# Scaling the features of linear attention on ScalarE or VectorE instead of GpSimd, with new due times for attention units, weights and raw unpacks

## The chip, the core and the metric

The kernel is one program on one core of a Trainium2 chip. The engines of a core run on their own and wait for one another by semaphores: TensorE (PE in the rows, PEld for its weight loads), VectorE (DVE), ScalarE (ACT), GpSimd (POOL) and SyncE (SP), which here issues the DMAs. The metric is device time in microseconds of one execution. Each engine works through its own list of instructions strictly in order.

## The reference

Three stages follow one another, all in float32. First linear attention with random features, over 4 batches and 8 heads of 576 tokens with 64 columns:

```python
def phi(x):                                   # 128 features
    proj = np.einsum('bhsd,md->bhsm', x, omega)
    h = proj - np.sum(x * x, axis=-1, keepdims=True) / 2.0
    h = h - np.max(h, axis=-1, keepdims=True)
    return np.exp(h) / np.sqrt(m)
kv = np.einsum('bhsm,bhsd->bhmd', k_p, v)
z = np.sum(k_p, axis=2)
num = np.einsum('bhsm,bhmd->bhsd', q_p, kv)
den = np.einsum('bhsm,bhm->bhs', q_p, z)[..., None] + 1e-06
return num / den
```

Its output becomes 2304 tokens of 512 columns. Then come two feed-forward layers, 512 to 2048 to 512 columns each: the first with `g = max(0.01 h, h)`, the second with `g = h * clip(h + 3, 0, 6) / 6`.

## The kernel before

**Tiling.** The 2304 tokens are worked on in five groups, 512, 256, 512, 512 and 512 tokens. Attention is cut into units: a K unit (`K_unit`) makes the key side of one batch and one pair of heads, a Q unit (`Q_unit`) the output of some tokens of one batch for one to four pairs of heads. Group 0's attention runs first. After that the first layer of a group (`moe1`) fills TensorE, and the units of later groups are slipped in between its matmuls, up to about 330 us. The rest of the time belongs to the two layers: float32 products made of three matmuls of split operands (L520, L521, L522), and in the second layer seven products in place of eight (L1199 for its hidden values, L1096 for its output).

**A Q unit.** Scores on TensorE (L775) give one bank of up to four blocks of 128 tokens by 128 features. VectorE takes minima (L740) and corrects them (L743, L745), ScalarE makes the exponentials into a tile `h` (L750), VectorE the denominators (L942) and their reciprocals (L948). Then `h` is scaled by the reciprocals, which stand one to a token, that is one to a partition and block: the step of this change, the op behind `sc` at L953. TensorE transposes the scaled blocks (L968), ScalarE or VectorE copies them out as `tq`, and a last product with `kvf` (L999) gives the output, copied to `xr`.

**A K unit.** Scores and exponentials as above, then `kvt` (L842) into a bank, copied out as `kvf`, transposed on TensorE (L849), copied again. Beside it the sums over tokens: GpSimd or VectorE adds halves of the `h` tiles in place (L509), then the 64 tokens left over (L862), and TensorE spreads the sum over the partitions (L866) for a copy to `zr`.

**Weights of the first layer.** They arrive packed and are unpacked by ScalarE (L550, L554) and VectorE (L552, L557, L560, L563). Each unpacked tile is split in a rounded part and a rest: a cast on ScalarE (L501) or GpSimd (L570), and a subtraction on VectorE (L504) or GpSimd (L505).

**What sets the order.** The code hands every step to a graph as an op with a due time, an estimated cost and one or more alternatives, each an engine with its cost. `Graph.run` then writes the program: it picks, over and over, the op that can start first by its own books, the one due earlier where two are close, and on the alternative that ends first. For ops of attention on TensorE a number is added to the time from which they may go: `WAIT` by the kind of op where the last matmul was one of the first layer's, `MATE` where it was itself a score ("S") or a 64-column product ("N"), `FOLLOW` behind an "F" op. The due time of an attention unit is its place in its group's stretch plus an entry of `MOVE_A` times 100 ns; `MOVE_W` does the same for the weights of the first layer, `MOVE_R` for the unpacking of the second layer's weights, which is done ahead of time. None of these numbers is in the program that runs; they decide only in which order, and on which engine, its instructions stand.

The op that scales, as it stands, with its two alternatives and their costs:

```python
g.op([("dve", c_dve(w), lambda sc=sc: sc(nc.vector), True), ("pool", 150 + w * 1.85, lambda sc=sc: sc(nc.gpsimd))],
     rd=[den], wr=[h], due=due + 4e3)
```

Of the kernel before, what the change touches and what calls it, by code (L numbers as in the profile page):

```python
# [13 lines left out]
AF = mybir.ActivationFunctionType  # L14
# [5 lines left out]
B, H, S, D = 4, 8, 576, 64  # L20
# [15 lines left out]
ST1, ST2 = 2, 2  # L36
SLACK = 1.0
PACE = 2.215
WAIT = {"S": 2250.0, "N": 1650.0, "F": 1300.0}
FOLLOW = 160.0  # L40
MATE = 60.0
TURN = {("M", "S"): 193.0, ("M", "N"): 92.0, ("S", "M"): 205.0, ("N", "M"): 158.0, ("F", "S"): 193.0, ("F", "N"): 97.0, ("S", "F"): 175.0,
        ("N", "F"): 150.0, ("S", "N"): 97.0, ("N", "S"): 150.0, ("F", "M"): 8.0}
OLDKV = 1
# [7 lines left out]
T0 = 42000.0  # L52
L1 = [100000.0, 52000.0, 127000.0, 87e3, 87e3]
ATT = [None, (32000.0, 132000.0), (132e3, 170000.0), (182e3, 244000.0), (220e3, 260000.0)]
MOVE_A = [[3, 9, -6, -16, 1, 25, 4, 21, 18],
# [4 lines left out]
MOVE_W = [-92, -14, -44, 44, 0, -14, 76, 43, -6, -11, -19, 86, -6, 15, -14, 7, 1, 28, 3, -3, -98, 56, 0, 18, -96, 40, 27, 0, 0, -1, 47, 0]  # L60
MOVE_R = [0, 26, -85, 43, -11, 44, 10, 154, 0, 0, 0, -67, 18, 42, -47, -62, 12, -5, -71, 66, 0, 106]
RAW = (142000.0, 302000.0)
PREP = (315000.0, 400000.0)
EARLYX = [0, 2, 3]
# [277 lines left out]
def c_dve(n):  # L342
    return n / 0.96 + 69.0
# [6 lines left out]
def c_act(n, psum=False, ap=False):  # L350
    return n / 1.2 + (51.0 if psum else 93.0) + (93.0 if ap else 0.0)
# [15 lines left out]
def attn_moe_kernel(ctx: ExitStack, tc: tile.TileContext, qT, kT, qn, kn, v1, om2, w1i, w1o, w2i, w2o, out):  # L367
# [4 lines left out]
    nc = tc.nc  # L372
    scale = float(D) ** -0.25
    g = Graph()
# [544 lines left out]
    def Q_unit(grp, b, hps, f, half, s0, col0, o, due):  # L919
        n, nh = f * 128 + 64 * half, len(hps)  # L920
        ncol, N, F = 2 * f + half, nh * n, f * 128
# [12 lines left out]
        for bank, (h, c) in enumerate(zip(hs, cols)):  # L934
            den, jk = Buf("den"), Buf("junk")
# [3 lines left out]
            def dn(h=h, den=den, jk=jk, heads=heads):  # L939
                for q, (k, _, e) in enumerate(heads):  # L940
# [8 lines left out]
                 wr=[den], due=due + 4e3)  # L949

            def sc(eng, h=h, den=den, c=c):
                x = h.tiles[0][:, 0:c * 128].rearrange("p (c f) -> p c f", f=128)
                eng.tensor_tensor(out=x, in0=x, in1=den.tiles[1][:, 0:c].to_broadcast([128, c, 128]), op=ALU.mult)  # L953

            w = c * 128
            g.op([("dve", c_dve(w), lambda sc=sc: sc(nc.vector), True), ("pool", 150 + w * 1.85, lambda sc=sc: sc(nc.gpsimd))],
                 rd=[den], wr=[h], due=due + 4e3)

            def tr(h=h, heads=heads):
                for q, (k, i, e) in enumerate(heads):  # L960
# [13 lines left out]
             wr=ts, also=[tq], due=due + 5e3)  # L974
# [5 lines left out]
        elif f:  # L980
            g.op(copy_alts(lambda: tq.tiles[0][:, :, 0:N], lambda: ts[0].tiles[0].rearrange("p (e n) -> p e n", e=2)[:, :, 0:N], 2 * N, True),
                 rd=[ts[0]], wr=[(tq, 0)], due=due + 5e3)
# [500 lines left out]
```

## Time and profile before

| what | value |
|---|---|
| median of three runs | 859.67 us (859.39 to 860.69) |
| the profiled execution | 860.87 us, its span 859.1 us |
| granted TensorE clock | 0.999 of full speed |
| TensorE matmuls | busy 849.7 us, 99%, 6279 of them |
| VectorE | busy 664.2 us, 77% |
| ScalarE | busy 511.0 us, 59% |
| GpSimd | busy 193.9 us, 23% |

Busy time says how long an engine had an instruction in work, not that someone waited for it. Who waited for whom is in two other views: the chain of the work that ended last, followed back from the end of the program, and the list of each engine's idle times with what ended them. A timeline row gives the start in us, the duration in us, engine, line and operation, the tiles (output first) and their shapes, how many instructions were put together, and in brackets the idle time before it with what ended it.

### The profile page before, as it was taken

How to read it: one execution, taken by the hardware profiler on the slowest of the kernel's cores; microseconds unless marked ns; L12 is line 12 of the kernel's file. 1: busy time of each engine (PE TensorE's matmuls, PEld its weight loads, DVE VectorE, ACT ScalarE, POOL GpSimd, SP SyncE). 2: the span in 40 equal slices, each digit the busy share in tenths (PEclk: the TensorE clock that was granted, in tenths of full speed). 3: DMA queues.
4: the chain of work that ended last, by engine and by line, in shares of the span. 5: the costliest groups of instructions: out<-in, count | busy, mean ns of one | idle time of the engine just before them, and what ended most of it. 6: DMA issues, size and time to landing. Idle time of an engine off the chain costs nothing.

```text
span 859.1 us, 18037 instructions
## 1 busy us (share of the span) xinstructions
PE 849.7 (99%) x6279; PEld 778.0 (91%) x6279; DVE 664.2 (77%) x1725; ACT 511.0 (59%) x1161; POOL 193.9 (23%) x279
## 2 busy tenths in 40 slices
PE   9999999999999999999999999999999999999998
PEld 8987888889888878888888889999999999999998
DVE  5999898966997965666889757886678779868765
ACT  6988797886877655544654455544443554345442
POOL 0125563333225321000100002122002223322110
PEclk9999999999999999999999999999999999999999
DMA  9566563766558416999888829986896784686441
GB/s 337 180 188 220 190 207 124 254 220 201 178 170 265 141 63 207 332 337 325 321 269 293 281 74 296 316 284 218 297 329 211 232 276 148 193 289 216 155 145 46
DMA packets 110250, 193.83 MB, mean 226 GB/s; under 512 B 13520, under 2 KB 46416, under 8 KB 110160
## 3 DMA queue, kind: packets, MB, share of 16 engines
q1 hardware_dynamic: 110016, 192.55, 68.1%
q8 instruction: 50, 0.82, 0.4%
q14 instruction: 40, 0.33, 0.1%
q10 hardware_dynamic: 144, 0.13, 0.1%
HBM read 148.60 MB, written 44.04 MB: 224 GB/s over the span
## 4 chain that ended last, share of the span: by engine, by line
PE 92%; DVE 3%; DMA 2%; ACT 1%; POOL 1%; issue 1%; DVEq 0%; POOLq 0%; SPq 0%; ACTq 0%
PE bank L1096 19%; PE bank L1199 17%; PE bank L520 15%; PE bank L522 14%; PE bank L521 14%; PE bank L775 4%; PE bank L999 2%; PE bank L842 2%; PE bank L968 1%; DVE junk L942 1%; PE bank L820 1%; PE bank L894 1%; DMA late_w<-in 1%; PE bank L866 1%; PE bank L1397 1%; DMA first_xn<-kn 1%
## 5 line engine op out<-in xcount | busy, mean ns | idle before, releaser
L501 ACT COPY late_u<-bank 128x256 f32<-128x256 f32 (+1 forms) x94 | 36.4, 387 | 79.0 <-PE bank L1199 74.6
L1096 PE MATMUL bank<-w,g 128*128 128x256 f32 x612 | 80.8, 275 | 0.0
L1096 PEld LDWEIGHTS bank<-w,g 128*128 128x128 f32 x612 | 74.4, 192 | 0.1
L1199 PE MATMUL bank<-w,late_w 128*128 128x256 f32 x546 | 72.9, 275 | 0.9 <-DMA late_w<-in 0.9
L1038 DVE TENSOR_TENSOR g<-bank,g 128x512 fp32r<-128x512 f32 (+1 forms) x80 | 50.4, 634 | 29.4 <-ACT g L501 28.5
L750 ACT ACTIVATE h<-bank,nm 128x128 f32<-128x128 f32 x228 | 63.7, 391 | 14.2 <-DVE nm L745 9.3
L1199 PE MATMUL bank<-x,late_w 128*128 128x256 f32 x540 | 69.3, 275 | 0.0
L1199 PEld LDWEIGHTS bank<-w,late_w 128*128 128x128 f32 x546 | 67.0, 192 | 1.3 <-DMA late_w<-in 1.1
L520 PE MATMUL bank<-x,w 128*128 128x512 f32 (+1 forms) x180 | 67.1, 373 | 0.0
L520 PE MATMUL bank<-g,w 128*128 128x512 f32 (+1 forms) x180 | 67.0, 372 | 0.0
L1199 PEld LDWEIGHTS bank<-x,late_w 128*128 128x128 f32 x540 | 64.9, 192 | 0.2
L1036 ACT ACTIVATE bank<-bank 128x512 f32<-128x512 f32 (+1 forms) x80 | 44.1, 553 | 34.8 <-PE bank L522 34.5
L522 PE MATMUL bank<-g,w 128*128 128x512 f32 (+1 forms) x180 | 64.6, 359 | 0.2 <-DVE g L1038 0.2
L522 PE MATMUL bank<-x,w 128*128 128x512 f32 (+1 forms) x180 | 64.6, 359 | 0.0
L521 PE MATMUL bank<-x,w 128*128 128x512 f32 (+1 forms) x180 | 64.5, 358 | 0.0
L521 PE MATMUL bank<-g,w 128*128 128x512 f32 (+1 forms) x180 | 64.5, 358 | 0.0
L1096 PE MATMUL bank<-second_w,g 128*128 128x256 f32 x453 | 59.9, 275 | 0.0
L740 DVE TENSOR_REDUCE nm<-bank 128x4 f32<-128x512 f32 (+2 forms) x76 | 47.2, 656 | 11.1 <-PE bank L775 9.9
L1096 PEld LDWEIGHTS bank<-second_w,g 128*128 128x128 f32 x453 | 55.2, 192 | 0.0
L501 ACT COPY u<-bank 128x256 f32<-128x256 f32 (+1 forms) x59 | 24.2, 412 | 51.8 <-PE bank L1199 30.8
L953 POOL TENSOR_TENSOR h<-h,den 128x512 f32<-128x512 f32 (+2 forms) x32 | 33.1, 1038 | 71.8 <-DVE den L948 44.0
L504 DVE TENSOR_TENSOR g<-xr,g 128x512 fp32r<-128x512 f32 (+1 forms) x55 | 36.7, 667 | 11.5 <-ACT g L501 10.4
(394 smaller groups left out, 2375.4 us busy)
## 6 DMA issues: line engine op xcount, KB each, us to landing
late_w<-in SPq DMA_DIRECT2D x207, 256.0 KB, 3.9
in<-late_w SPq DMA_DIRECT2D x64, 256.0 KB, 3.8
third_w<-in SPq DMA_DIRECT2D x49, 256.0 KB, 4.0
wst<-w2i SPq DMA_DIRECT2D x16, 512.0 KB, 4.7
wst<-w2o SPq DMA_DIRECT2D x16, 512.0 KB, 4.3
x_t<-late_w SPq DMA_DIRECT2D x12, 512.0 KB, 4.6
wst<-w1o SPq DMA_DIRECT2D x11, 512.0 KB, 3.6
v<-v SPq DMA_DIRECT2D x14, 330.0 KB, 4.2
```

The source lines that it names most:

```text
L501: return [("act", c_act(n, psum), lambda: nc.scalar.copy(dst(), src())), dve if psum else dve + (True,)]
L504: return [("dve", c_dve(n), lambda: nc.vector.tensor_tensor(out=dst(), in0=src(), in1=hi().bitcast(F32), op=ALU.subtract), True), ("pool", ...
L520: nc.tensor.matmul(o, lhsT=ah, rhs=bh, start=start, stop=False)
L521: nc.tensor.matmul(o, lhsT=al, rhs=bh, start=False, stop=False)
L522: nc.tensor.matmul(o, lhsT=ah, rhs=bl, start=False, stop=stop)
L740: g.op([("dve", c_dve(c * 128), lambda raw=raw, n_=n_: nc.vector.tensor_reduce(out=n_()[:, :, 0], in_=raw(), axis=AX.X, op=ALU.min))], rd= ...
L750: nc.scalar.activation(h.tiles[0][:, q * 128:q * 128 + 128], raw()[:, q], AF.Exp, bias=nm.tiles[0][:, q], scale=-1.0)
L775: nc.tensor.matmul(ps[e].tiles[0][:, at:at + 128], lhsT=src.tiles[0][r, k * one + i * 128:k * one + i * 128 + 128], rhs=wn[r], start=True, ...
L1036: g.op([("act", c_act(n, True), lambda: nc.scalar.activation(P(), P(), AF.Prelu, alpha=0.01))], wr=[p], due=d)
L1038: g.op([("dve", c_dve(n), lambda: nc.vector.tensor_tensor(out=G1(), in0=P(), in1=G0().bitcast(F32), op=ALU.subtract))], rd=[p, (gg, 0)], w ...
L1096: nc.tensor.matmul(acc[bank].tiles[0][:, half * 256:half * 256 + 256], lhsT=src.tiles[x][:, q * 128:q * 128 + 128], rhs=woven(w[k].tiles[y ...
L1199: nc.tensor.matmul(R[r](), lhsT=w[x], rhs=m[y], start=start and k == n == 0, stop=k == 1 and n == 2, skip_group_check=True)
```

## The change

The scaling gets a new second alternative. In place of GpSimd, which scaled the whole tile by one instruction with a broadcast operand, ScalarE may do it by one activation (`Copy` with a scale per partition) for each 128 columns. VectorE's alternative stays. Three constants of the planner and all of `MOVE_A`, `MOVE_W` and `MOVE_R` get other values; two rows of `MOVE_A` stand here for the rest.

```diff
-WAIT = {"S": 2250.0, "N": 1650.0, "F": 1300.0}
+WAIT = {"S": 1850.0, "N": 1600.0, "F": 1350.0}
 FOLLOW = 160.0
-MATE = 60.0
+MATE = 520.0
...
-MOVE_A = [[3, 9, -6, -16, 1, 25, 4, 21, 18],
-          [-30, 9, -29, 9, 9, -9, -79, 38],
+MOVE_A = [[-124, -103, -86, -78, -48, 31, -14, 4, -2],
+          [-31, -4, -37, 2, -6, -12, 0, -28],
...
-            g.op([("dve", c_dve(w), lambda sc=sc: sc(nc.vector), True), ("pool", 150 + w * 1.85, lambda sc=sc: sc(nc.gpsimd))],
-                 rd=[den], wr=[h], due=due + 4e3)
+            def by_act(h=h, den=den, c=c):
+                for q in range(c):
+                    x = h.tiles[0][:, q * 128:q * 128 + 128]
+                    nc.scalar.activation(x, x, AF.Copy, scale=den.tiles[1][:, q])
+
+            g.op([("dve", c_dve(w), lambda sc=sc: sc(nc.vector), True), ("act", c * c_act(128, True, True), by_act)], rd=[den], wr=[h], due=due + 4e3)
```

Of the 32 scalings, all on GpSimd before, 26 are on ScalarE now, as 90 activations (L959), and 6 on VectorE (L953). The lines behind the new function stand four further down: L968 is L972, L999 is L1003, L1038 is L1042, L1096 is L1100, L1199 is L1203. The number of matmuls is the same.

In the rows below the names carry slot and copy numbers: `w7_90` is slot 7 of the first layer's split weights, `late_w0_1` a weight tile of the second layer that is fetched while the layer runs.

First, SyncE's queue for the second layer, at about 594 us in the trace of before. Before:

```order
L693 DMA late_w0_1_0_3819<-in_3_0_256_243 128x512
L693 DMA late_w0_1_0_3819<-in_3_1_0_244 128x512
L525 DMA xr1_0_113<-x1_4_0_77 128x2x256
L693 DMA late_w0_2_0_3820<-in_3_1_256_245 128x512
L693 DMA third_w2_0_0_1645<-in_3_2_0_246 128x512
L525 DMA late_xr3_1_0_3829<-x1_4_0_77 128x2x256
L525 DMA xr3_0_115<-x1_4_1_78 128x2x256
L693 DMA late_w0_0_0_3818<-in_3_3_256_249 128x512
```

and of the changed kernel:

```order
L693 DMA late_w0_1_0_3883<-in_3_0_256_243 128x512
L525 DMA xr1_0_113<-x1_4_0_77 128x2x256
L525 DMA late_xr3_1_0_3893<-x1_4_0_77 128x2x256
L693 DMA late_w0_1_0_3883<-in_3_1_0_244 128x512
L693 DMA late_w0_2_0_3884<-in_3_1_256_245 128x512
L693 DMA third_w2_0_0_1691<-in_3_2_0_246 128x512
L525 DMA xr3_0_115<-x1_4_1_78 128x2x256
L693 DMA late_w0_0_0_3882<-in_3_3_256_249 128x512
```

The loads of `xr1` and `late_xr3` moved ahead of the second fetch into `late_w0_1`; the rest of the piece kept its order.

Second, GpSimd's queue around the first K unit of group 1, at about 60 to 70 us in the trace of before; a minus marks rows of before, a plus rows of the changed kernel:

```order
 L505 TENSOR_TENSOR w5_88<-first_wt6_1_0_175,w5_88 128x512
-L953 TENSOR_TENSOR h0_0_145<-h0_0_145,den2_1_193 128x512
-L505 TENSOR_TENSOR w6_89<-wt0_0_110,w6_89 128x512
+L570 CAST w6_89<-wt0_0_110 128x512
 L570 CAST w7_90<-wt1_0_111 128x512
+L570 CAST w8_91<-first_wt6_0_0_174 128x512
+L570 CAST w9_92<-first_wt6_1_0_175 128x512
 L509 TENSOR_TENSOR h1_0_146<-h1_0_146 128x256
 L509 TENSOR_TENSOR h2_0_147<-h2_0_147 128x256
```

A scaling and a subtraction ahead of the K unit's additions are gone from GpSimd, and three casts stand there beside the one of before.

Third, TensorE at the K unit that makes `kvf2`. Before, the last rows ahead of its transpose, of which the unit's `kvt` (L842) stands five rows above the first:

```order
L521 MATMUL bank6_182<-x1_102,w12_95 128x256
L522 MATMUL bank6_182<-x1_102,w12_95 128x256
L520 MATMUL bank6_182<-x2_103,w12_95 128x256
L521 MATMUL bank6_182<-x2_103,w12_95 128x256
L522 MATMUL bank6_182<-x2_103,w12_95 128x256
L520 MATMUL bank6_182<-x3_104,w12_95 128x256
L521 MATMUL bank6_182<-x3_104,w12_95 128x256
L522 MATMUL bank6_182<-x3_104,w12_95 128x256
L520 MATMUL bank0_176<-g0_105,w11_94 128x256
L521 MATMUL bank0_176<-g0_105,w11_94 128x256
L522 MATMUL bank0_176<-g0_105,w11_94 128x256
L849 MATMUL bank4_180<-ident_184,kvf2_0_130 128x128
```

and of the changed kernel:

```order
L842 MATMUL bank3_179<-h1_0_146,v0_0_144 64x128
L842 MATMUL bank3_179<-h2_0_147,v0_0_144 64x128
L842 MATMUL bank3_179<-ht0_0_152,v0_0_144 64x128 x2
L1003 MATMUL bank0_176<-tq0_0_154,kvf1_0_129 64x384 x2
L849 MATMUL bank3_179<-ident_184,kvf2_0_130 128x128
L520 MATMUL bank5_181<-g2_107,w9_92 128x256
```

Between `kvt` and the transpose of its result stood fifteen matmuls of the first layer, and now one group of two.

Fourth, ScalarE's queue at the same place in the changed kernel:

```order
L501 COPY tq0_0_154<-bank3_179 128x384
L1040 ACTIVATE bank0_176<-bank0_176 128x256
L501 CAST g0_105<-bank0_176 128x256
L554 ACTIVATE wt1_0_111<-wst1_0_109 128x512
L550 ACTIVATE wst1_0_109<-wst1_0_109 128x512
L501 COPY kvf2_0_130<-bank3_179 128x128
```

The copy that the transpose reads, `kvf2`, has two unpacking steps of a weight directly ahead of it.

## Rows read from the trace of the kernel before

**Rows 1.** The chain that ended last, share of the span by engine.

```profile
PE 92%; DVE 3%; DMA 2%; ACT 1%; POOL 1%; issue 1%; DVEq 0%; POOLq 0%; SPq 0%; ACTq 0%
```

**Rows 2.** TensorE's waits: line, releaser, total us, times, longest us.

```profile
PE bank L1199 <- DMA late_w<-in: 0.9, 1, 0.9
PE bank L1096 <- DVE late_g L504: 0.5, 1, 0.5
PE bank L849 <- ACT kvf L501: 0.4, 1, 0.4
...
PE bank L522 <- DVE g L1038: 0.2, 1, 0.2
PE bank L520 <- ACT tq L501: 0.2, 1, 0.2
```

**Rows 3.** Busy us (instructions) by stretch: PE, PEld, DVE, ACT, POOL, clock, DMA, GB/s.

```profile
58.00:160.00 102.00, 101.35 (x643) 84.35 (x642) 93.08 (x225) 86.68 (x194) 49.38 (x55) 1.00 0.59 191
...
592.00:594.00 2.00, 2.00 (x21) 2.00 (x20) 1.23 (x4) 1.65 (x3) 0.00 (x0) 1.00 0.54 186
```

**Rows 4.** The group of scalings: count, busy us, mean ns, idle before and its releaser.

```profile
L953 POOL TENSOR_TENSOR h<-h,den 128x512 f32<-128x512 f32 (+2 forms) x32 | 33.1, 1038 | 71.8 <-DVE den L948 44.0
```

**Rows 5.** ScalarE groups from 55 to 300 us, and one timeline row of eight exponentials.

```profile
L750 ACT ACTIVATE h<-bank,nm 128x128 f32<-128x128 f32 x188 | 52.4, 387 | 12.6 <-DVE nm L745 8.6 <-DVE nm L743 3.8
...
L554 ACT ACTIVATE wt<-wst 128x512 f32<-128x512 f32 x26 | 21.4, 822 | 2.8 <-DMA wst<-w2i 1.7 <-DMA wst<-w2o 0.5 <-DVE tq L500 0.4
...
176.23 2.19 ACT L750 ACTIVATE h<-bank,nm 128x128 f32<-128x128 f32 x8
```

**Rows 6.** VectorE's and GpSimd's timeline around 98.9 us.

```profile
98.68 0.32 DVE L942 CUSTOM_DVE_ANT_0 junk<-h,zr 128x128 bf16<-128x128 f32 x1
...
98.93 1.17 DVE L942 CUSTOM_DVE_ANT_0 junk<-h,zr 128x128 bf16<-128x128 f32 x1
...
98.23 0.62 POOL L570 CAST second_w<-stage_wt 128x512 fp32r<-128x512 f32 x1
98.91 1.05 POOL L953 TENSOR_TENSOR h<-h,den 128x512 f32<-128x512 f32 x1
```

**Rows 7.** The chain in order of time behind an L999 group: start, us, what.

```profile
63.42 0.41 PE bank L520
63.83 0.22 PE bank L521
```

**Rows 8.** VectorE's timeline, the last read of `xr1`.

```profile
590.26 0.69 DVE L504 TENSOR_TENSOR g<-xr,g 128x512 fp32r<-128x512 f32 x1 [0.89 <-ACT g L501]
```

**Rows 9.** SyncE's timeline, the two loads that moved.

```profile
594.38 0.56 SPq L525 DMA_DIRECT2D xr<-x  x1
...
596.16 1.30 SPq L525 DMA_DIRECT2D late_xr<-x  x1
```

**Rows 10.** The chain in order of time at 607 us.

```profile
603.13 5.71 DMA late_w<-in
```

**Rows 11.** Timelines at the first K unit of group 1: TensorE, GpSimd, ScalarE, VectorE.

```profile
69.94 0.33 PE L849 MATMUL bank<-ident,kvf 128*128 128x128 f32 x1 [0.35 <-ACT kvf L501]
...
72.49 0.38 PE L522 MATMUL bank<-x,w 128*128 128x512 f32 x1
72.99 0.70 PE L866 MATMUL bank<-zr,ones 128*128 128x256 f32 x2
...
66.94 3.42 POOL L509 TENSOR_TENSOR h<-h 128x256 f32<-128x256 f32 x2 [1.70 <-PE bank L842]
...
69.63 0.26 ACT L501 COPY kvf<-bank 128x128 f32<-128x128 f32 x1
...
68.40 0.67 DVE L563 SCALAR_TENSOR_TENSOR first_wt<-first_wt,wst 128x512 uint32<-128x512 uint32 x1
```

**Rows 12.** TensorE's and ScalarE's timeline behind a kvt with ScalarE free.

```profile
197.00 0.70 PE L866 MATMUL bank<-zr,ones 128*128 128x256 f32 x2
...
197.11 0.27 ACT L501 COPY kvf<-bank 128x128 f32<-128x128 f32 x1 [1.57 <-PE bank L842]
```

More of the change, by code (lines that the diff above doesn't have):

```diff
@@ L54 @@
 ATT = [None, (32000.0, 132000.0), (132e3, 170000.0), (182e3, 244000.0), (220e3, 260000.0)]
-MOVE_A = [[3, 9, -6, -16, 1, 25, 4, 21, 18],
[4 rows of a table removed]
-MOVE_W = [-92, -14, -44, 44, 0, -14, 76, 43, -6, -11, -19, 86, -6, 15, -14, 7, 1, 28, 3, -3, -98, 56, 0, 18, -96, 40, 27, 0, 0, -1, 47, 0]
-MOVE_R = [0, 26, -85, 43, -11, 44, 10, 154, 0, 0, 0, -67, 18, 42, -47, -62, 12, -5, -71, 66, 0, 106]
+MOVE_A = [[-124, -103, -86, -78, -48, 31, -14, 4, -2],
[4 rows of a table added]
+MOVE_W = [90, 1, -30, 118, 3, -4, 76, 35, -23, 0, -77, 152, 34, 18, 74, 0, -5, 13, -14, -23, -157, -39, -29, -21, -55, 57, -8, 0, -4, -34, 116, 14]
+MOVE_R = [-7, -52, -46, 25, -55, 38, 2, -179, 33, 19, 68, 216, -111, 224, 30, -15, -39, -85, -245, 1, 0, -71]
 RAW = (142000.0, 302000.0)
```

6 rows, old and new, of the table MOVE_A are left out of this document.

## The prediction

> **What bounds the kernel now.** I read the chain of work that ended last first. TensorE has 92% of it, the rest is crumbs [rows 1]. So a scaling taken off GpSimd is worth only what TensorE waited because of it, and the second view is the list of TensorE's waits with the releaser of each [rows 2]. None names the scaling or the transposes L968 that read its result. What stands there, before the list's last two crumbs: 0.9 us for a late weight tile in the second layer (L1199), 0.5 us for a subtraction at L1096 near the end, 0.4 us for the copy ahead of a K transpose (L849). A few waits in the first 58 us are left out of the rows, since the order of TensorE, VectorE, ScalarE and GpSimd is the same in both kernels up to there. The third view is busy time by stretch: between 58 and 160 us, the densest stretch of attention, TensorE works 101.35 us of 102.00, ScalarE 86.68, VectorE 93.08, GpSimd 49.38 [rows 3]. GpSimd, which the change relieves, was the emptiest engine there, and VectorE the one nearest to full. There is little to win, and the question is which small wait goes and which comes.
>
> **The change part by part.** The profiled execution took 860.87 us with a span of 859.1, the median of the runs is 859.67. The sum is made against 860.87 and the same difference is then taken from 859.67; the two differ by 1.2 us, as one execution does from another.
>
> *The scaling.* Out go 32 GpSimd instructions, 33.1 us in all [rows 4]. In come 6 on VectorE and 26 groups on ScalarE, of 90 activations of 128 columns. The nearest row is the exponentials, the same 128x128 shape with a pointer operand: eight in 2.19 us, so the pitch is about 0.26 us [rows 5], and 90 take 23.4 us of ScalarE, spread over some 250 us. In the dense stretch ScalarE had 15 us idle [rows 3], and it also hands back some casts and unpacks: it issues 7 casts of 512 columns fewer, 6 fewer L550 and 3 fewer L554. On TensorE's path I price this at 0. The cover is the matmuls of the first layer, which stand in TensorE's order between a unit's scores and its transposes; where it is gone, the price is the rival below. GpSimd's freed time partly goes to 8 more casts of 512 columns at 0.62 us each [rows 6]. VectorE gains too where it no longer meets the scaling: a denominator L942 took 0.32 us alone and 1.17 us when a scaling on GpSimd had begun 0.02 us before it [rows 6]. VectorE is on no wait of attention in [rows 2], so this is 0 as well.
>
> *Turns of shape.* Between matmuls of the first layer and attention's narrower ones TensorE loses time: in the chain the first 512-column piece after an L999 group takes 0.41 us and the next 0.22 [rows 7], so 0.19 us for one turn. TensorE's order has 112 changes of shape before and 110 after: 2 x 0.19 = 0.4, taken as **-0.4** (0 to -0.4).
>
> *The late weight tile at 607 us.* After about 300 us all engines run the same sequence of lines in both kernels, except on SyncE's queue: two loads, of xr1 and late_xr3, stood behind a fetch of late_w0_1 and stand before it now (the first order shown). The last read of xr1's slot, VectorE's L504, is over at 590.95 us [rows 8], but the loads issue at 594.38 and 596.16 [rows 9]: the fetch ahead waited for its slot. Between 592 and 594 us the DMA engines were 0.54 busy [rows 3]. Put ahead, the loads go some 2 us earlier into that room and leave the later queue emptier. The fetch on which TensorE waits 0.9 us was issued at 603.13 and landed 5.71 us later [rows 10]. Bounds: 0, if it waits for its own slot whatever is queued, and -1.04, which the two waits around it come to with the restart. The shift of the loads is twice the wait, so I take **-1.0**.
>
> *The first K unit of group 1* is the one place where the new order on GpSimd touches a chain that ends at TensorE. There TensorE waits about 0.5 us at L849, 0.35 of it for the copy kvf that ended at 69.89, and is late again by about 0.3 before L866 at 72.99, which needs GpSimd's additions L509 from 66.94 on and L862 behind them [rows 11]. In the new order the casts w6 to w9 stand ahead of these additions (the second order shown), and w9's must wait for VectorE's L563, done at 69.07 [rows 11]. On TensorE the unit's kvt (L842) stands 6 matmuls later, L849 and L866 at the same distance behind it. Lower end: both waits go, -0.8. Upper end: VectorE has one more subtraction ahead, 0.69 [rows 8], then the cast 0.62 [rows 6]: 69.07 + 0.69 + 0.62 = 70.38; the additions would be allowed from 66.94 + 6 x 0.22 = 68.26, so they start 2.1 us late, **+2.1**. I take **+0.8**, nearer to the middle: the row of VectorE shows w9's input 2 us behind kvt, but only one of the four casts must wait for it.
>
> On this place the trace has a row: with a GpSimd instruction begun 0.02 us before it, a denominator of VectorE took 0.85 us longer [rows 6]. The Trainium skill, "SBUF — State Buffer", section Summary: rules for kernel authors, says of a VectorE instruction with two SBUF inputs and a GpSimd instruction that reads SBUF that the second is blocked until the first is done; the row agrees. By that rule L563, which has two inputs in SBUF, could be held for one of the added casts, and this term's upper end would be +2.7 in place of +2.1; the sum goes by +2.1.
>
> *Two K transposes that have lost their distance.* Before, 15 matmuls stand between a unit's kvt and its transpose; in the new order kvf2's transpose has one L999 group of two in between (the third order shown), and kvf0's about three groups of three. The copy in between costs 0.4 us when ScalarE is free: kvt is over at 197.00, the copy runs 197.11 to 197.38 [rows 12]. Lower end 0, since the two L999 cover that. Upper end: ScalarE has an L554 and an L550 directly ahead of that copy (the fourth order shown), 0.82 us by L554's mean [rows 5] and as much again for L550, **+1.6** for kvf2, and **+1.0** for kvf0, where one such instruction and the copy may be in front. Taken **+0.4** together: two 0.8 us instructions have mostly run by the time the unit's kvt ends, since ScalarE's previous rows are casts that TensorE's earlier matmuls released.
>
> *Small waits that may fall away*: 0.2 us at L520 (tq) and 0.2 at L522 (g) [rows 2] stand where the new order has other neighbours. Bounds 0 and -0.7, with the restart behind each and the one at 69 us left out; taken **-0.2**. The 0.5 us at L1096 lies where nothing moved: 0.
>
> Sum: 0 - 0.4 - 1.0 + 0.8 + 0.4 - 0.2 = **-0.4 us**: 860.87 becomes 860.5 for a profiled execution, 859.67 becomes **859.3** for the median.
>
> **The rivals.** *All attention waits go (faster).* The new due times remove what is listed between 58 and 330 us and bring nothing: -0.4 - 1.0 - 0.8 - 0.7 = -2.9, 856.8 us. For it: every wait there is one late copy or addition behind unlucky neighbours. Against: the two orders above that look worse, not better.
>
> *ScalarE's queue stands behind the denominators (slower).* A scaling on ScalarE waits for VectorE's reciprocal, and what is queued behind it are the first layer's g and the copies tq and kvf, for which TensorE waits. Before, ScalarE's exponentials wait 12.4 us in 47 groups of four for VectorE's minima [rows 5], 0.27 us a group. At half of that a group, 26 groups hold ScalarE 3.4 us more; it decides from the point where one of the copies behind them is the next thing TensorE wants. All of it on the path gives 859.3 + 3.4 = 862.7. Against: L968 reads the scaled tile, and no wait for it is in [rows 2] with GpSimd's slower scaling. The Trainium skill is on this rival's side: "ScalarE: Activation LUTs", section Rules for kernel authors, sends a plain multiply to VectorE and not to ScalarE; by that rule the 26 groups lie on the wrong engine. No run of before shows a scaling on either of the two.
>
> *K units at their upper ends (slower).* GpSimd's casts at +2.1, kvf2's transpose at +1.6: -0.4 - 1.0 + 2.1 + 1.6 = +2.3, 862.0.
>
> *The wait at 607 stays.* The fetch was held by its own slot: 0.6 us above before, 860.3.
>
> That the change does not do what it says is excluded by the order: no scaling is left on GpSimd.
>
> **How the numbers follow.** Forecast 0.46 (its own range 858.2 to 860.5), all waits gone 0.26, ScalarE's queue 0.12, K units 0.10, the wait at 607 stays 0.06. A measurement of this kernel tells about 0.2% from no change, 1.7 us, so faster is below 857.95 and slower above 861.39. Faster: 0.26 and 0.02 of the forecast, 0.28. Slower: 0.12 + 0.10 = 0.22. Same: the rest, 0.50. The range reaches from the fast rival with L1096's 0.5 gone too, 856.3, to the slow one at 862.7; about half of each end's rival lies outside.
>
> **What would show it.** Right: L1199's 0.9 us is gone and the fetch before 608 us is issued earlier; no wait of TensorE for a tile scaled at L953 or L959; a wait of about 1 us at L866 or L849 near 68 to 75 us; ScalarE's sum up by 10 to 20 us, GpSimd's down by about as much as 33 minus its casts. Wrong: a wait for a copy of tq, g or kvf whose engine row shows a scaling directly ahead of it; a wait at L1199 or L1096 as before; any new wait over 2 us in the dense stretch. What could break the forecast altogether is a place that I have not priced, since nearly every row between 58 and 300 us has new neighbours.

## The result, and the profile after

The changed kernel is slower: 866.08 us median of seven executions (865.38 to 870.71) against 859.99 for before, a ratio of 1.0083 with a 95% interval of 1.0069 to 1.0096. By that ratio it is 7.1 us slower (the two medians lie 6.1 us apart), where 0.4 us less was forecast, and the median lies 3.4 us above the upper end of the range. The executions of the changed kernel lie in two groups, four from 865.4 to 866.1 and three from 869.5 to 870.7; the first trace is of the upper group (870.71, span 868.9), and a second one was taken of another execution, which took 867.18 and belongs to neither group. How far the traces explain the two groups is part of the answer below.

The page of the first trace: busy time by engine, then the chain by engine [rows 1].

```profile
PE 854.4 (98%) x6279; PEld 780.4 (90%) x6279; DVE 661.7 (76%) x1740; ACT 523.8 (60%) x1235; POOL 166.1 (19%) x254
...
PE 80%; DVE 9%; ACT 7%; issue 2%; POOL 1%; DMA 1%; SPq 0%; DVEq 0%; ACTq 0%
```

TensorE has 80% of the chain instead of 92%: at some places it is now led by VectorE and ScalarE. TensorE's largest waits of the changed kernel behind the first 58 us, in the columns of [rows 2]:

```profile
PE bank L866 <- POOL zr L862: 3.8, 1, 3.8
...
PE bank L520 <- ACT h L750: 0.5, 2, 0.4
PE bank L1100 <- DVE late_g L504: 0.5, 1, 0.5
PE bank L522 <- DVE x L504: 0.4, 1, 0.4
PE bank L849 <- ACT kvf L501: 0.4, 1, 0.4
```

The wait at the weight tile near 607 us (L1199 before, L1203 now) is gone, as forecast. At the top stands the place that the prediction had named and sized at +0.8: L866 of the first K unit of group 1, which waits for GpSimd's sums. Then the stretches, in the columns of [rows 3]:

```profile
58.00:160.00 102.00, 97.14 (x581) 79.55 (x579) 87.73 (x198) 75.85 (x178) 46.19 (x50) 0.97 0.54 172
...
74.00:78.40 4.40, 0.59 (x3) 0.19 (x1) 1.62 (x3) 1.79 (x3) 4.31 (x6) 0.93 0.42 140
78.50:83.40 4.90, 4.90 (x11) 3.46 (x11) 1.89 (x3) 1.48 (x3) 1.58 (x2) 0.50 0.11 23
```

From about 74.6 to 78.4 us TensorE stands idle, and for the next 5 us its granted clock is 0.50, the lower of its two levels, 1.2 GHz in place of 2.4. The single rows, TensorE first, then GpSimd, then VectorE; [rows 11] is the same place before:

```profile
74.21 0.38 PE L522 MATMUL bank<-g,w 128*128 128x512 f32 x1
78.44 1.22 PE L866 MATMUL bank<-zr,ones 128*128 128x256 f32 x2 [3.85 <-POOL zr L862]
...
79.88 0.63 PE L521 MATMUL bank<-g,w 128*128 128x512 f32 x1
80.31 0.63 PE L522 MATMUL bank<-g,w 128*128 128x512 f32 x1
...
66.72 1.35 POOL L570 CAST w<-first_wt 128x512 fp32r<-128x512 f32 x1
70.66 0.89 POOL L570 CAST w<-first_wt 128x512 fp32r<-128x512 f32 x1 [2.60 <-DVE first_wt L563]
71.52 4.66 POOL L509 TENSOR_TENSOR h<-h 128x256 f32<-128x256 f32 x2
76.14 1.31 POOL L509 TENSOR_TENSOR zr<-h 128x128 f32<-128x128 f32 x2
...
69.92 0.69 DVE L563 SCALAR_TENSOR_TENSOR first_wt<-first_wt,wst 128x512 uint32<-128x512 uint32 x1
...
71.59 0.67 DVE L504 TENSOR_TENSOR w<-wt,w 128x512 fp32r<-128x512 f32 x1
72.19 0.68 DVE L504 TENSOR_TENSOR w<-first_wt,w 128x512 fp32r<-128x512 f32 x1
```

It is the chain that the prediction's upper end had worked out: w9's cast waits 2.60 us for L563, starts at 70.66 and holds the additions back until 71.52, though kvt has been over since 69.2. What the prediction did not have is what follows. The two additions take 4.66 us instead of 3.42, the wait becomes 3.85 us, and the matmuls behind it come 0.43 us apart where 0.22 is their pitch.

### The profile page after: what moved, and what is told of

Its sections match the earlier page's. It is cut to its first block, busy times and chain, and to the rows that moved or that the text cites. A ratio compares the mean times of both kernels' runs of the same rounds, so it can differ in the third digit from the quotient of the medians.

```text
span 868.9 us, 18069 instructions
## 1 busy us (share of the span) xinstructions
PE 854.4 (98%) x6279; PEld 780.4 (90%) x6279; DVE 661.7 (76%) x1740; ACT 523.8 (60%) x1235; POOL 166.1 (19%) x254
## 4 chain that ended last, share of the span: by engine, by line
PE 80%; DVE 9%; ACT 7%; issue 2%; POOL 1%; DMA 1%; SPq 0%; DVEq 0%; ACTq 0%
PE bank L1100 19%; PE bank L1203 17%; PE bank L520 12%; PE bank L521 12%; PE bank L522 12%; PE bank L775 3%; DVE nm L740 1%; PE bank L842 1%; ACT h L750 1%; DVE g L1042 1%; PE bank L1003 1%; ACT h L959 1%; DVE wt L563 1%; PE bank L972 1%; PE bank L820 1%
## 5 line engine op out<-in xcount | busy, mean ns | idle before, releaser
L1100 PE MATMUL bank<-w,g 128*128 128x256 f32 x612 | 80.8, 275 | 0.0
L1042 DVE TENSOR_TENSOR g<-bank,g 128x512 fp32r<-128x512 f32 (+1 forms) x80 | 50.7, 636 | 31.3 <-ACT g L501 29.1
L1100 PEld LDWEIGHTS bank<-w,g 128*128 128x128 f32 x612 | 74.4, 192 | 0.1
L1203 PE MATMUL bank<-w,late_w 128*128 128x256 f32 x546 | 73.0, 275 | 0.1
L750 ACT ACTIVATE h<-bank,nm 128x128 f32<-128x128 f32 x228 | 63.9, 397 | 11.3 <-DVE nm L745 5.3
L1203 PE MATMUL bank<-x,late_w 128*128 128x256 f32 x540 | 69.3, 275 | 0.0
L520 PE MATMUL bank<-g,w 128*128 128x512 f32 (+1 forms) x180 | 68.4, 380 | 0.2 <-ACT h L750 0.2
L1203 PEld LDWEIGHTS bank<-w,late_w 128*128 128x128 f32 x546 | 67.1, 192 | 0.5 <-DMA late_w<-in 0.3
L520 PE MATMUL bank<-x,w 128*128 128x512 f32 (+1 forms) x180 | 66.5, 370 | 0.4 <-ACT h L750 0.4
L521 PE MATMUL bank<-g,w 128*128 128x512 f32 (+1 forms) x180 | 65.2, 362 | 0.0
L522 PE MATMUL bank<-g,w 128*128 128x512 f32 (+1 forms) x180 | 65.2, 362 | 0.0
L522 PE MATMUL bank<-x,w 128*128 128x512 f32 (+1 forms) x180 | 64.7, 359 | 0.4 <-DVE x L504 0.4
L1203 PEld LDWEIGHTS bank<-x,late_w 128*128 128x128 f32 x540 | 64.9, 192 | 0.2
L740 DVE TENSOR_REDUCE nm<-bank 128x4 f32<-128x512 f32 (+2 forms) x76 | 47.5, 657 | 16.9 <-PE bank L775 12.3
L1100 PE MATMUL bank<-second_w,g 128*128 128x256 f32 x453 | 59.9, 275 | 0.0
L1100 PEld LDWEIGHTS bank<-second_w,g 128*128 128x128 f32 x453 | 55.2, 192 | 0.0
L504 DVE TENSOR_TENSOR g<-xr,g 128x512 fp32r<-128x512 f32 (+1 forms) x55 | 36.7, 667 | 11.5 <-ACT g L501 10.4
L520 PE MATMUL bank<-x,second_w 128*128 128x512 f32 (+1 forms) x120 | 43.9, 365 | 0.3 <-POOL second_w L570 0.3
```

Of the source, the lines that this page charges most:

```text
L504: return [("dve", c_dve(n), lambda: nc.vector.tensor_tensor(out=dst(), in0=src(), in1=hi().bitcast(F32), op=ALU.subtract), True), ("pool", ...
L520: nc.tensor.matmul(o, lhsT=ah, rhs=bh, start=start, stop=False)
L521: nc.tensor.matmul(o, lhsT=al, rhs=bh, start=False, stop=False)
L522: nc.tensor.matmul(o, lhsT=ah, rhs=bl, start=False, stop=stop)
L740: g.op([("dve", c_dve(c * 128), lambda raw=raw, n_=n_: nc.vector.tensor_reduce(out=n_()[:, :, 0], in_=raw(), axis=AX.X, op=ALU.min))], rd= ...
L750: nc.scalar.activation(h.tiles[0][:, q * 128:q * 128 + 128], raw()[:, q], AF.Exp, bias=nm.tiles[0][:, q], scale=-1.0)
```

## The experiments

Each run replays the recorded order of one of the two kernels, engine by engine and buffer by buffer, with the stated edit and no new planning, so that one thing changes at a time. The excess is the ratio to before in the same series, less one, times 860 us, with its 95% interval.

| run | excess over before, us |
|---|---|
| the changed kernel | +7.1 (5.9 to 8.3) |
| before_scale_act: order of before, scaling as changed | +6.3 (5.1 to 7.5) |
| before_scale_dve: order of before, all on VectorE | +2.8 (1.8 to 3.9) |
| before_act_fill: before, and 90 idle activations | +13.8 (12.6 to 15.0) |
| before_no_scale: before without the scalings | +0.4 (-0.3 to 1.2) |
| after_scale_pool: new order, all on GpSimd | +13.0 (11.3 to 14.7) |
| after_scale_dve: new order, all on VectorE | +13.7 (12.3 to 15.0) |
| after_w9_act: changed, w9's cast on ScalarE | +4.1 (3.0 to 5.2) |
| after_w9_late: changed, w9's cast behind the additions | +6.2 (5.0 to 7.4) |
| after_busy: changed, TensorE busy through the wait | +7.3 (6.1 to 8.4) |
| after_k_split: changed, half of the additions on VectorE | +3.0 (1.8 to 4.2) |
| after_k_split_no_scale: the same without the scalings | +2.1 (1.2 to 2.8) |
| before_sp_swap: before, two loads moved | -0.7 (-1.5 to 0.1) |
| before_tidy: before, five instructions moved | -0.6 (-1.4 to 0.2) |
| before_tidy_split: the same, and half of the additions on VectorE | -2.0 (-2.8 to -1.1) |

### Scaling alone and order alone

```diff
 # before_scale_act: the order of before
-POOL L953 h <- h, den   (32, whole tiles)
+ACT  L959 h <- h, den   (26 groups, 90 pieces), DVE L953 (6)
 # after_scale_pool: the order of the changed kernel
-ACT  L959 (26 groups), DVE L953 (6)
+POOL L953 (32)
```

> The order of before, instruction by instruction, with only the engine of the 32 scalings changed as the change does it: 26 on ScalarE as 90 activations, 6 on VectorE, at the same places of the order. Two theories. K theory (the loss comes from the new order, above all from GpSimd's casts ahead of the first K unit's additions): no wait at L866 near 73 us beyond before's 0.3 us, time 859 to 861.5, within 0.2% of before. ScalarE theory (activations that wait for reciprocals hold up the copies behind them): 862.5 to 867, with waits of TensorE for ACT tq, kvf or g whose row on ScalarE shows L959 directly ahead.

> The order of the changed kernel, instruction by instruction, with all 32 scalings put back on GpSimd at their places. K theory: the wait for zr at L866 stays or grows (one more scaling stands ahead on GpSimd), so 865 to 872, no better than the changed kernel. ScalarE theory: most of the loss is gone, 860 to 863.

Both came out high, so neither theory holds alone. In the old order the new scaling costs 6.3 us, and the new order with the old scaling costs 13.0 us, more than the two together cost in the changed kernel. In the trace of after_scale_pool TensorE waits 2.5 us for g from VectorE (L522), 2.3 at L866 and 2.2 for casts of GpSimd's queue (L520). TensorE's waits in before_scale_act, with the scaling alone changed:

```profile
PE bank L849 <- ACT kvf L501: 1.2, 1, 1.2
PE bank L1003 <- ACT tq L501: 1.1, 2, 0.6
```

TensorE now waits for copies of tq and kvf on ScalarE. The wait for kvf is not the scaling's, though. Ahead of that copy stands w9's cast, which waits for VectorE's L563; L563 took 0.67 us before [rows 11] and takes 1.22 here, beside GpSimd's additions. ScalarE, then VectorE in before_scale_act:

```profile
70.77 0.62 ACT L501 CAST w<-first_wt 128x512 fp32r<-128x512 f32 x1 [1.95 <-DVE first_wt L563]
...
69.52 1.22 DVE L563 SCALAR_TENSOR_TENSOR first_wt<-first_wt,wst 128x512 uint32<-128x512 uint32 x1
```

The run without any scaling, before_no_scale, has the same wait of TensorE:

```profile
PE bank L849 <- ACT kvf L501: 1.3, 1, 1.3
```

As the order is that of before, the starts of TensorE's matmuls can be compared one by one in the two traces. At 330 us TensorE is 6.6 us behind before. Of this 0.7 us came with a wait for tq at 63 us, 0.5 at this K unit and 3.6 between 140 and 180 us, at waits for tq, h, g and xr; 1.0 us is won back at 607 us.

In the trace of before_scale_act, the view of line L959 says how long ScalarE was idle ahead of the scalings, and how often:

```profile
  DVE den L948: 1.8, 2
```

ScalarE itself waits for the reciprocals only 1.8 us in the whole run. So the waiting that the rival had priced is too small for the loss.

### What ScalarE's time costs

```diff
 # before_act_fill: before, at 26 places of ScalarE's order
+ACT  zero <- zero * 3.0   (128x128, as many pieces as the group has)
 # before_scale_dve, before_no_scale
-POOL L953 (32)
+DVE  L953 (32)            resp. nothing
```

> The kernel of before, scalings on GpSimd as they were, plus the same 90 activations on ScalarE that the change adds, at the same 26 places of its order, but on a tile of zeros that nobody waits for and that waits for nothing (output unused). It separates what ScalarE's time costs from what waiting for the denominators costs. Occupancy theory (the 0.3 us a piece displaces the copies of tq and kvf that stand behind): TensorE shows the waits of the run with the scalings moved, at L1003 near 160 us and L849 near 70 us, and the time is 864 to 867. Dependence theory (the loss comes from ScalarE standing in front of a reciprocal, or from the scaled tile being late): 859.5 to 861.5.

> The order of before with all 32 scalings on VectorE instead of GpSimd, at their places. 18 of 0.69 us, 12 of 0.56 and 2 of about 0.4 are 20 us on VectorE against 29.5 us that ScalarE's 90 activations took. If VectorE's queue displaces what TensorE waits for as ScalarE's does, and by its share of time: 20/29.5 of the 5.6 us, so about 864. If a multiply belongs on VectorE: 859 to 861.

> The kernel of before without the 32 scalings: the features stay undivided, so the output is the numerator alone. It gives the price of the scaling as it stood on GpSimd, and so the most that moving it anywhere could win. Cover theory (the scaling was hidden): 859 to 861. If GpSimd's 33 us and its holding up of VectorE cost TensorE time, 855 to 858.

Without any scaling the kernel of before takes as long as with it: on GpSimd the step was hidden, and in this order no place for it could have won more than the 0.3 us at the interval's end. The idle activations, which wait for nothing and for which nobody waits, cost 13.8 us, above the range that I had given. So occupancy is enough: time on ScalarE's in-order queue pushes back what stands behind it. TensorE's waits in that run:

```profile
PE bank L1003 <- ACT tq L501: 2.1, 4, 1.1
PE bank L866 <- POOL zr L862: 2.0, 2, 1.8
PE bank L972 <- DVE g L1042: 1.4, 2, 0.8
...
PE bank L775 <- ACT tq L501: 1.0, 1, 1.0
```

Why it costs more than the real scaling there (6.3) was not parted. The idle activations took 36.7 us of ScalarE where the scalings took 29.5; each of them reads and writes the tile of the one before it. And this run still has GpSimd's step behind the late denominators, ahead of L972. VectorE took the same work for 2.8 us in the old order. In its trace 2.0 us of waits are at L866, 1.8 of them at the first K unit, where GpSimd's additions took 7.3 us in place of 6.0; 0.8 more are at L1003 and L972, and the wait at 607 us is gone. The Trainium skill ("ScalarE: Activation LUTs", section Rules for kernel authors) would have a multiply on VectorE and not on ScalarE. In the old order the runs agree, 2.8 against 6.3. In the new order they do not: there ScalarE (7.1) is better than VectorE (13.7) and GpSimd (13.0). Which engine costs least depends on the order; that the new order was laid out for ScalarE is the likely reason, and no run parts it from others.

### The first K unit

```diff
 # after_w9_act
-POOL L570 w9 <- first_wt
+ACT  L501 w9 <- first_wt   (same place of the order)
 # after_w9_late: GpSimd's queue
-L570 w9 <- first_wt
 L509 h1, L509 h2, L509 zr, L509 zr, L862 zr, L862 zr
+L570 w9 <- first_wt        (and VectorE's L504 w9 later)
 # after_k_split
-POOL L509 h2 <- h2; L509 zr <- h2; L862 zr   (one of two each)
+DVE  the same three, at the same places
```

> The changed kernel with one instruction moved to another engine: the cast of weight tile w9 (128x512), which stands last ahead of the first K unit's additions on GpSimd, goes to ScalarE at the same place of the order. K theory: the additions start about 2.5 us earlier, right behind kvt, the wait at L866 falls from 3.85 us to under 1.5, TensorE's granted clock stays at its upper level behind it, and the time falls by 4 to 7 us, to 860.5 to 863. ScalarE theory, or any cause spread over the order: within 1 us of the changed kernel.

> The changed kernel with w9's cast moved on GpSimd from ahead of the first K unit's additions to behind them, its subtraction on VectorE moved behind accordingly; engines as in the changed kernel. K theory: the wait at L866 near 74 us is under 1 us and no wait comes in its place at L849 (as it did when the cast went to ScalarE), the clock stays up, and the time is 861.5 to 863.5, lower than with the cast on ScalarE (864.3). Otherwise 864 or more.

> The changed kernel with three of the first K unit's six additions moved from GpSimd to VectorE at the same places (one L509 of 256 columns, one of 128, one L862: 0.7 us of VectorE against some 2.7 us of GpSimd). K theory: GpSimd ends its half by 74 us, the wait at L866 is under 0.6 us, the clock stays up in all executions, and the time is 862 to 864, where the changed kernel has 865.4 to 870.7. If the loss is spread over ScalarE's queue alone, 865 or more.

All three take the wait at L866 away; the first two put another in its place and came out slower than expected, at 864.27 and 866.21 us. On ScalarE the cast waits for L563 as it did on GpSimd, and the copy kvf stands behind it. TensorE's wait in after_w9_act:

```profile
PE bank L849 <- ACT kvf L501: 1.6, 1, 1.6
```

and the two rows on ScalarE's timeline that make it:

```profile
71.40 0.62 ACT L501 CAST w<-first_wt 128x512 fp32r<-128x512 f32 x1 [0.27 <-DVE first_wt L563]
...
72.44 0.26 ACT L501 COPY kvf<-bank 128x128 f32<-128x128 f32 x1
```

In after_w9_late I had moved w9's subtraction too far down VectorE's queue, and TensorE's waits show it, near 80 us:

```profile
PE bank L521 <- DVE w L504: 1.9, 1, 1.9
```

So after_w9_late tells nothing of the size. The third moves no cast. The timeline of after_k_split, GpSimd's half of the additions and TensorE's L866:

```profile
69.03 0.89 POOL L570 CAST w<-first_wt 128x512 fp32r<-128x512 f32 x1 [3.31 <-DVE first_wt L563]
69.89 0.73 POOL L509 TENSOR_TENSOR h<-h 128x256 f32<-128x256 f32 x1
70.70 0.52 POOL L509 TENSOR_TENSOR zr<-h 128x128 f32<-128x128 f32 x1
71.30 0.45 POOL L862 TENSOR_TENSOR zr<-zr,ht 64x128 f32<-64x128 f32 x1
...
72.57 0.38 PE L522 MATMUL bank<-g,w 128*128 128x512 f32 x1
72.78 0.59 PE L866 MATMUL bank<-zr,ones 128*128 128x256 f32 x2
```

The cast still waits for L563, L866 no longer waits at all (VectorE's half of the additions took 1.9 us, where 0.7 was expected), the granted clock is 1.00 in all five executions, and the excess falls from 7.1 to 3.0 us. Between 60 and 86 us TensorE gains 7.3 us on the first trace of the changed kernel and 4.3 us on the second one; the other differences between these traces, up to 1.4 us before 20 us and 0.4 at 98 us among them, are smaller. The first K unit is the larger part of the loss.

### Why the executions differ, and the clock

```diff
 # after_busy: TensorE, ahead of the first L866 of group 1
+L1401 bank <- zero   (x22, 128x384, into the bank that L866 then overwrites)
```

> The changed kernel once more, for the trace of another execution. K theory with two outcomes: where GpSimd's additions L509 are held by VectorE (4.7 us for the two, as in the first trace) TensorE waits 3.9 us at L866 and its clock falls, 869 to 871; where they run freely (under 2.5 us for the two) the wait is 1.5 to 2.5 us, the clock stays up, 865 to 866.5.

> The changed kernel with 22 matmuls of zeros (384 columns, about 0.16 us each, 3.6 us in all) ahead of the first L866 of group 1, into the same bank, so that TensorE works through the wait for GpSimd. If the fall of the granted clock behind that wait comes from TensorE standing idle, every matmul behind it keeps its full-speed pitch (0.216 us for 512 columns instead of 0.427) and the executions of the changed kernel that show a clock below 1.0 lose 2.5 to 3 us: all executions at 864.5 to 867.5. If the slow matmuls have another cause, the pitch of 0.427 us stays between 78 and 83 us and nothing is won.

The timeline of the second trace of the changed kernel, GpSimd, VectorE, TensorE:

```profile
70.92 1.87 POOL L509 TENSOR_TENSOR h<-h 128x256 f32<-128x256 f32 x2
...
70.99 1.21 DVE L504 TENSOR_TENSOR w<-wt,w 128x512 fp32r<-128x512 f32 x1
72.12 1.21 DVE L504 TENSOR_TENSOR w<-first_wt,w 128x512 fp32r<-128x512 f32 x1
...
76.29 0.85 PE L866 MATMUL bank<-zr,ones 128*128 128x256 f32 x2 [2.30 <-POOL zr L862]
```

and the stretch behind that wait, in the columns of [rows 3]:

```profile
76.60:79.80 3.20, 3.20 (x9) 2.56 (x8) 1.92 (x4) 0.86 (x2) 1.04 (x2) 0.52 0.44 164
```

The granted clock is 0.52 in it, for 3 us; I had expected it to stay up where the additions run freely. The instructions and their order are those of the first trace, but the other engine is held: in the first trace the additions took 4.66 us and VectorE's subtractions 0.67 and 0.68, here the additions take 1.87 and the subtractions 1.21 each. In this trace the two engines end by turns, each some 0.55 us behind the other's end. In the first trace GpSimd's first addition alone took 3.98 us; it ended 0.59 us behind the last of five VectorE instructions that stood close together, of which this row is the last:

```profile
71.52 3.98 POOL L509 TENSOR_TENSOR h<-h 128x256 f32<-128x256 f32 x1
...
74.24 0.67 DVE L563 SCALAR_TENSOR_TENSOR wt<-wt,wst 128x512 uint32<-128x512 uint32 x1
```

The Trainium skill ("SBUF — State Buffer", section Summary: rules for kernel authors) says of a VectorE instruction with two SBUF inputs and a GpSimd one that reads SBUF that the second to issue is blocked until the first finishes. The second trace agrees. The first does not show it: there the addition began 0.07 us ahead of the first of the five, as it did in the second trace, and was held all the same. What decides is open; the two executions that were traced came out in the two ways. The four instructions behind the two additions win part of it back, so that the wait is 2.3 or 3.9 us.

This explains the two traces, and not all of the spread. None of the four executions from 865.4 to 866.1 us was traced. Three of them have a granted clock of 1.000 over the whole span and one 0.997, against 0.996 in the three of the upper group and 0.998 in the second trace. That a short wait without the lower clock makes the lower group fits these numbers and is not shown.

With TensorE kept at work through the wait, the granted clock stays at 1.00 in all four executions. The timeline of after_busy:

```profile
74.49 3.99 PE L1401 MATMUL bank<-zero 128*128 128x384 f32 x22
78.31 0.59 PE L866 MATMUL bank<-zr,ones 128*128 128x256 f32 x2
```

and the stretch that had 0.50 in the first trace:

```profile
78.50:83.40 4.90, 4.90 (x34) 4.05 (x34) 3.32 (x7) 1.48 (x3) 1.01 (x1) 1.00 0.38 125
```

From L866 to the next scores took 2.47 us here (78.31 to 80.78) and 4.99 in the first trace of the changed kernel (78.44 to 83.43), so the lower clock cost 2.5 us there. The run is not faster in all (7.3 against 7.1): its four executions took 866.7 to 868.7 us, where up to 867.5 had been expected. The zeros take their 3.8 us also where the sums are ready earlier; in this trace they were ready at 76.84 and L866 began at 78.31. Waits of about 2 us went both ways: 2.3 us in the second trace and 1.9 in after_w9_late were followed by the lower clock, 2.3 us in the trace of after_scale_pool was not.

### What is left, and a version below both

> The same, and the 32 scalings left out altogether (the features stay undivided, so the output is the numerator alone). The difference to the run with them is what the scaling on ScalarE costs in the new order. ScalarE theory: its 29 us on an in-order queue cost 2 to 4 us there, so 859.5 to 861.5. If the new order is slower by itself: within 1 us of the run with the scalings.

With the K unit mended, leaving out the scalings takes 0.9 us more, at the edge of what these runs part (1.0035 against 1.0024, intervals that overlap), and 2.1 us (1.2 to 2.8) remain that are neither the scaling nor the K unit. From 58 to 340 us TensorE is idle 2.5 us in that trace, and 0.8 in the trace of before. Its waits are many small ones, where before had three of 0.2 to 0.4 in attention [rows 2]:

```profile
PE bank L849 <- DVE g L1042: 0.6, 1, 0.6
...
PE bank L522 <- DVE x L504: 0.4, 1, 0.4
PE bank L520 <- ACT h L750: 0.4, 1, 0.4
...
PE bank L866 <- POOL zr L862: 0.3, 1, 0.3
PE bank L520 <- POOL second_w L570: 0.3, 1, 0.3
```

Which change of neighbours makes each of them was not tested.

> The order of the changed kernel with all 32 scalings on VectorE, where the changed kernel has 26 on ScalarE. The new order with GpSimd scaling took 872.4, with ScalarE 865.4 to 870.7. If ScalarE's queue carries much of the loss in the new order too (some 3 us of waits between 100 and 330 us), VectorE gives 861 to 864 or less; if the first K unit carries it, its wait at L866 stays and the time is 864 to 870.

With the scalings on VectorE the new order is slower still, at 13.7 us, beyond all that I had written down; the wait at L866 is there (2.2 us), and TensorE waits 2.4 us for g from VectorE, in four places. The layout has no room on VectorE.

```diff
 # before_sp_swap: SyncE
+DMA xr1; DMA late_xr3      ahead of the second fetch into late_w0_1
 # before_tidy: that, and
 DVE  L903 u1; L899; L901; L903 u1
+DVE  L560, L563            (were between them)
 ACT
+L501 kvf <- bank           ahead of w9's cast
 # before_tidy_split: that, and the three additions on VectorE as in after_k_split
```

> The kernel of before with only the two loads on SyncE's queue (xr1 and late_xr3) moved ahead of the second fetch into late_w0_1, as the changed kernel has them. If that order made TensorE's wait at 607 us, as the prediction said, the wait of 0.9 us is gone and the time is 0.7 to 1.1 us lower. If the wait comes from when the transfers fall together, it stays, moves to another fetch or goes without the order having to do with it, and the median is within 0.4 us of before.

> The kernel of before with five instructions moved in their queues: the two loads on SyncE as in the run with the swap; on VectorE an unpacking pair L560 and L563 behind the last L903 that TensorE's 1.3 us wait at L912 near 46 us is for; on ScalarE the copy kvf of the first K unit ahead of w9's cast, which waits for VectorE. If TensorE's waits at 46, 69 and 607 us are each set by the order of one queue, 1.3, 0.5 and 0.9 us go and the median is 857 to 858.5; if what stands next is only a little later, 858.5 to 860.

> The tidied kernel of before (five instructions moved) with the first K unit's additions shared in the same way. The tidied kernel's executions spread from 858.0 to 862.4, and its trace has a wait of 2.0 us at L866, where GpSimd's two L509 took 3.8 us. If that is all that came in place of the waits taken away, it goes, and the median is 856.8 to 858.2, below both kernels, with the spread under 1.5 us. If something else is next, 858.5 to 860.

The swap alone is not parted from nothing (859.79 against 860.67; 0.9992, 0.9983 to 1.0001), though its median lies where the first reading put it. The wait at 607 us is gone in it, and one of 0.3 us for another fetch is there, near 525 us. The tidied kernel had lost its waits at 46, 69 and 607 us, but the trace has 2.0 us at L866 in their place, and its executions spread from 858.0 to 862.4. With the additions shared out it is 858.65 (858.1 to 859.5), 0.9977 of before with an interval of 0.9967 to 0.9987: the one version here that lies clearly below both kernels, if by less than I had expected. Its waits of TensorE in attention over 0.3 us:

```profile
PE bank L522 <- DVE g L1042: 0.7, 2, 0.5
...
PE bank L521 <- DVE third_w L504: 0.4, 1, 0.4
```

## Why the prediction was wrong, point by point

By the runs the 7.1 us divide into 4.1 for the first K unit, about 0.9 for the scaling and 2.1 for all else that the new order changed. The sum of the prediction had +0.8, 0 and -1.2 in their places.

- **What bounds the kernel** was read rightly: TensorE, with waits of a few tenths, and the scaling on none of them. before_no_scale shows it: there was nothing to win. That such a kernel has little to lose as well stands in no row; the prediction took it for granted, and it was false.
- **The first K unit, +0.8 between -0.8 and +2.1, is the step that failed most.** The mechanism and the place were right, and nearly the start: the additions were to start 2.1 us late and started 2.4 us late (71.52, with kvt over at 69.2). The size was wrong three times over. I took a value in the middle, though the row of L563 put w9's input behind kvt and nothing in the order let it come earlier. I kept the additions' length, though [rows 6] show what GpSimd and VectorE do to each other (even the 0.32 us there is not "alone", as GpSimd's cast ran until 98.85); 1.87 or 4.66 us is the spread. And I priced no clock: behind the waits of 2.3 and 3.9 us TensorE ran 3 and 5 us at 1.2 GHz, which cost 2.5 us in the first trace. after_k_split puts the whole at 4.1 us (7.1 less 3.0), counted against a unit almost without waits.
- **The scaling, priced at 0,** was the second. In the new order it costs about 0.9 us, at the edge of what can be told; in the old order it would have cost 6.3. The cover that I named was not one: the matmuls between scores and transposes hide the scaling itself, not the copies behind it on ScalarE: in before_scale_act TensorE waits for tq. The slower rival had the right engine, but priced its waits for reciprocals (3.4 us from half of 0.27 a group), and those came to 2.4 us of ScalarE, none of them shown to reach TensorE. Occupancy alone is enough to cost time, as before_act_fill shows, and it was sized too low: 90 pieces took 29.3 us, not 23.4.
- **The late weight tile, -1.0:** the wait went, 1.0 us, as said. But it also went in before_scale_act, before_no_scale, before_act_fill and before_scale_dve, whose queue on SyncE is that of before, and waits of 0.3 to 0.9 us at another fetch near 535 us came in four variants of the changed kernel. The order of the two loads is not shown to be the cause; when the transfers fall together is as good a reading. Before was traced once, so whether the wait belongs to most of its executions is not known either.
- **The K transposes, +0.4:** kvf2's and kvf0's L849 follow their L1003 group 0.42 and 0.47 us after its last start, about 0.2 us each beyond a free follow-on. Right in size, in the first trace.
- **The turns, -0.4, and the small waits, -0.2:** not measured apart. The new order brings its own small waits, 2.1 us with all else taken out, where the prediction took -0.6 for the two terms together. Their single causes stay open. This is the place that the last sentence of the prediction left open, "nearly every row between 58 and 300 us has new neighbours", and it should have had a price with a sign: TensorE had only 0.8 us of idle time left there, so new neighbours had little to win and much to add.
- **The chances:** 0.22 for slower was too little. Both slower rivals came true in part at once, and the range held each of them alone.

## What to carry to other kernels

Where one engine is at 99% and leaving a step out altogether wins nothing, as here, moving that step has nothing to win, and its price is set by what stands behind it in the new engine's in-order queue, not by that engine's idle share. Leaving the step out is the first run to make: it gives the most that another placement can win in the same order. A wait of a few microseconds on TensorE should be priced with the slower matmuls that can follow it, and an order laid out for one engine should not be judged with the work on another.

## What the runs showed of the hardware that I had not expected

- The same program, in the same order, ran GpSimd's two additions of 128x256 in 1.87 us in one execution and in 4.66 in another, with VectorE's subtractions beside them at 1.21 and 0.67 us; in both the first addition began 0.07 us ahead of the subtraction. With the clock behind it this place makes 3.1 of the 3.9 us between the spans of the two traces (865.0 and 868.9).
- TensorE's granted clock was 0.50 for 5 us behind a wait of 3.85 us and 0.52 for 3 us behind one of 2.30 us; it stayed at 1.00 behind a wait of 2.30 us in after_scale_pool, and where matmuls of zeros filled the first wait.
- 90 activations of 128x128 on ScalarE that touch nothing anyone needs cost the kernel 13.8 us. They took 36.7 us of ScalarE, which had 15 us of idle time in the dense 102 us.
